# First batch of a decay attention from key-major to query-major tiles, ahead of two feed-forward layers

## The chip, the cores and the metric

The kernel runs on one core of one Trainium2 chip. The metric is device time in microseconds (us), the median of three runs; lower is better. The five instruction queues are PE (TensorE, with its weight loads PEld), DVE (VectorE), ACT (ScalarE), POOL (GpSimd) and SP, which here issues all transfers. Each works through its own list in order.

## What is computed

Four batches of eight heads, 576 tokens, 64 values a head. Attention with a decay and a causal mask is followed by two feed-forward layers on 2304 tokens of 512 values, with 2048 hidden columns each:

```python
scores = scale * np.matmul(q, k.transpose(0, 1, 3, 2))
cum = np.cumsum(np.log(np.clip(f, 0.0001, 1.0)), axis=-1)
decay = cum[:, :, :, None] - cum[:, :, None, :]
scores = np.where(causal, -1000000000.0, scores + decay)
attn = np.exp(scores - np.max(scores, axis=-1, keepdims=True))
attn = attn / (np.sum(attn, axis=-1, keepdims=True) + 1e-09)
x = np.matmul(attn, v)              # then tokens x 512
h = x @ w_in;  g = np.maximum(h, 0.0) + alpha * np.minimum(h, 0.0);  x = g @ w_out
h = x @ w2_in; g = where(h >= 1, h, where(h <= -1, 0, (h + 1) ** 2 / 4)); out = g @ w2_out
```

The inputs q and k are drawn some 29 times larger than a unit scale would ask for, so the scores spread widely, and the row maximum has to be subtracted. The weights come as 64-bit floats.

## The kernel before, in words

**Units.** The attention of a batch is cut into two units: unit 0 holds queries 0 to 255, unit 1 queries 256 to 575 (`QA = 256`). In a unit the eight heads go in four pairs (`pr`). Units 0 and 1, the first batch, are called plain (`plain = u < 2`): their products are fp32 products. The later batches split each operand into a high and a low fp32r part and run each product as two or three fp32r products.

**One head of a plain unit, key-major.** Q and K of the pair are transposed on PE (L573, L538) and copied out by ACT (L582, L546), so that the head's 64 values lie along partitions. L668 multiplies a block of 128 keys with all queries of the unit: a score tile is 128 keys by up to 320 queries. Unit 0 has two such blocks (256 and 128 queries wide, by causality), unit 1 five (320, 320, 320, 192, 64). ACT evacuates each block with the decay of the key as a per-partition bias (L686), POOL masks the diagonal block (L476). The row maximum runs over keys, so along partitions: DVE takes the maximum of the blocks (L707, L725), POOL reduces it over the partitions (L731), DVE subtracts (L747), ACT exponentiates (L752). Keys lie along partitions already, so L787 multiplies V with the probabilities without a transpose. The 64 columns between the two heads of V in `vF` are ones, which gives the sum of each query in a row of the output.

**The normalization.** ACT takes sums and outputs out of PSUM (L829, L830). For each pair SP gathers the sums into 128 partitions (L849), DVE inverts them (L853, L854), SP writes them to DRAM (L857) and reads them back spread over 64 partitions twice (L861), DVE multiplies (L871), and the result is split into its high and low part of x (ACT L881, DVE L884).

**Weights.** `convert` turns each of the 32 pieces of the first layer's 64-bit weights into a high and a low fp32r part: ACT L929, DVE L932, L941, L949, L954, ACT L962, DVE L967, all on 128 x 512. The last two pieces use a buffer of their own (`val1`), one after the other.

**The first layer.** Tokens go in nine chunks of 256, hidden columns in 16 slices. `l1_slice` has twelve products h (L1014), a chain ACT L1024, DVE L1027, ACT L1033, DVE L1036, and twelve products y (L1053) that accumulate over the slices in PSUM; L1068 takes a finished chunk out. Slice s needs the pieces 2s and 2s+1. Chunk 0 needs unit 0 of the first batch, chunk 1 unit 1.

**The order.** Every step is a task with an engine, a cost, a position and its dependencies. `Order.emit` writes the tasks out: at each step it takes the engine that can start first by the planner's own costs, and on it the task with the lowest position (`pos_of` for attention, `l1_pos` for the layer; conversions start 9 positions ahead of their slice). What is written is fixed: on the chip each engine keeps to that order. `phase2` marks the opening of the buffers for the split batches (`open_phase(2)`); it depends on all plain V products and on all 32 conversions:

```python
if u == 2 and pr == 0:
    phase2 = add("X", 0, lambda: open_phase(2), -50, plain_pv + ["convert"])
```

## Time and profile before

| | |
|---|---|
| median of three runs | 1054.39 us |
| lowest and highest | 1053.09 and 1056.34 us |
| profiled execution, first to last instruction | 1054.7 us |
| busy in that span: PE, DVE, ACT, POOL | 1013.4, 752.7, 656.6, 142.0 us |

The profiled execution shows its span, 1054.7 us, as its own time; nothing lies around it that the rows would have to explain. Busy time is the sum of instructions on an engine with overlaps counted once. A span is better read by stage than as a whole, since PE is busy nearly throughout after the first 150 us and is not before.

### The profile page before, as it was taken

What the parts mean: (1) busy time and instruction counts of PE and PEld (TensorE: products, weight loads), DVE (VectorE), ACT (ScalarE), POOL (GpSimd) and SP (SyncE); (2) the same over time, 40 slices, a digit from 0 to 9 for tenths busy, and PEclk for the clock granted to TensorE, in tenths of its full rate; (3) what the DMA queues carried; (4) which work ended last, traced back from release to release, by engine and by line L of the source; (5) the groups of instructions that cost most, each with busy time, mean ns of one, the idle gap of its engine ahead of it and who ended that gap; (6) DMA issues with size and microseconds to landing.
All of it is one profiled execution on the core that took longest, in us unless ns stands there. A gap on an engine that the chain in (4) does not pass through costs nothing.

```text
span 1054.7 us, 18462 instructions
## 1 busy us (share of the span) xinstructions
PE 1013.4 (96%) x6147; PEld 905.4 (86%) x6147; DVE 752.7 (71%) x1899; ACT 656.6 (62%) x1732; POOL 142.0 (13%) x239
## 2 busy tenths in 40 slices
PE   5869979999999999999999999999999999999998
PEld 3548779999999999999999888988888888888886
DVE  7999997888778777787756999974454455444443
ACT  6978867988988788887854655652333343333333
POOL 3422321212331122311200000000000000000000
PEclk9889989999999999999999999999999999999999
DMA  8674422321133111331104454530011001000001
GB/s 229 156 216 113 130 62 55 71 50 49 38 73 72 37 49 38 69 76 37 39 7 129 143 155 148 173 89 32 1 41 40 1 1 40 1 1 31 11 1 40
DMA packets 125071, 72.22 MB, mean 68 GB/s; under 512 B 89360, under 2 KB 118032, under 8 KB 124976
## 3 DMA queue, kind: packets, MB, share of 16 engines
q1 hardware_dynamic: 124976, 71.04, 24.7%
q8 instruction: 49, 0.80, 0.3%
q14 instruction: 46, 0.38, 0.2%
HBM read 61.42 MB, written 9.51 MB: 67 GB/s over the span
## 4 chain that ended last, share of the span: by engine, by line
PE 79%; ACT 7%; DVE 6%; issue 3%; DMA 3%; SPq 1%; POOL 1%; ACTq 0%; POOLq 0%; DVEq 0%
PE ps_h L1287 19%; PE ps_z L1334 19%; PE ps_h L1014 11%; PE ps_y L1053 11%; PE ps_y L1141 4%; PE ps_h L1097 4%; PE ps_s L672 3%; PE ps_o L787 2%; DMA raw<-in_moe_w_in_dram 2%; PE ps_o L793 1%; ACT S L686 1%; ACT S L752 1%; PE ps_o L795 1%; PE ps_o L794 1%; DVE kT L558 1%
## 5 line engine op out<-in xcount | busy, mean ns | idle before, releaser
L1014 PE MATMUL ps_h<-x,w 128*128 128x256 f32 x1344 | 185.3, 288 | 2.4 <-DVE g L1027 2.4
L1053 PE MATMUL ps_y<-gH,w 128*128 128x256 f32 x896 | 184.7, 289 | 0.1
L1287 PE MATMUL ps_h<-xw,w 128*128 128x512 f32 x768 | 184.5, 389 | 0.0
L1334 PE MATMUL ps_z<-w,gH 128*128 128x512 f32 x576 | 177.6, 389 | 0.0
L1014 PEld LDWEIGHTS ps_h<-x,w 128*128 128x128 f32 x1344 | 171.4, 193 | 3.6 <-DVE g L1027 3.5
L1287 PEld LDWEIGHTS ps_h<-xw,w 128*128 128x128 f32 x768 | 144.2, 188 | 29.9
L1312 ACT CAST gH<-g 128x256 fp32r<-128x256 f32 x144 | 58.6, 407 | 166.8 <-PE ps_z L1334 163.3
L1315 DVE TENSOR_TENSOR gL<-g,gH 128x256 fp32r<-128x256 f32 x144 | 61.1, 424 | 128.8 <-ACT gH L1312 128.6
L1053 PEld LDWEIGHTS ps_y<-gH,w 128*128 128x128 f32 x896 | 147.6, 191 | 0.6 <-ACT gH L1033 0.3
L1053 PE MATMUL ps_y<-gL,w 128*128 128x256 f32 x448 | 127.6, 285 | 0.4 <-DVE gL L1036 0.2
L1334 PEld LDWEIGHTS ps_z<-w,gH 128*128 128x128 f32 x576 | 107.2, 188 | 21.5
L1304 ACT ACTIVATE g<-g,half 128x256 f32<-128x256 f32 x144 | 73.2, 509 | 66.4 <-DVE g L1300 66.3
L1334 PE MATMUL ps_z<-w,gL 128*128 128x512 f32 x288 | 112.0, 389 | 0.0
L686 ACT ACTIVATE S<-ps_s,nb 128x320 f32<-128x320 f32 (+3 forms) x224 | 99.6, 449 | 19.3 <-PE ps_s L672 15.6
L476 POOL TENSOR_SCALAR_AFFINE_SELECT S<-S 128x128 f32<-128x128 f32 (+1 forms) x160 | 61.4, 388 | 313.9 <-ACT S L686 262.4
L731 POOL PARTITION_ALL_REDUCE Mb<-Mx x64 | 79.1, 1237 | 77.3 <-ACT Mx L715 43.2
L1307 DVE TENSOR_TENSOR g<-ps_h,g 128x256 f32<-128x256 f32 x144 | 60.9, 424 | 38.8 <-ACT g L1304 38.2
L1053 PEld LDWEIGHTS ps_y<-gL,w 128*128 128x128 f32 x448 | 85.9, 192 | 1.7 <-DVE gL L1036 1.1
L752 ACT ACTIVATE S<-S 128x320 f32<-128x320 f32 (+1 forms) x192 | 79.4, 424 | 12.0 <-DVE S L747 11.2
L747 DVE TENSOR_TENSOR S<-Mb,S 128x320 f32<-128x320 f32 (+3 forms) x224 | 77.5, 397 | 7.0 <-POOL Mb L731 6.0
L787 PE MATMUL ps_o<-S,vF 128*128 128x64 f32 (+4 forms) x256 | 67.4, 357 | 8.8 <-DMA vF<-in_v_dram 4.5
L1027 DVE SCALAR_TENSOR_TENSOR g<-g,calpha,ps_h 128x256 f32<-128x256 f32 x112 | 53.0, 476 | 28.7 <-ACT g L1024 28.2
(112 smaller groups left out, 1799.9 us busy)
## 6 DMA issues: line engine op xcount, KB each, us to landing
raw<-in_moe_w_in_dram SPq DMA_DIRECT2D x32, 512.0 KB
raw<-in_moe_w_out_dram SPq DMA_DIRECT2D x32, 512.0 KB
x<-x SPq DMA_DIRECT2D x9, 512.0 KB
out_dram<-osb SPq DMA_DIRECT2D x18, 256.0 KB
qr<-in_q_dram SPq DMA_DIRECT2D x64, 64.0 KB
raw<-in_k_dram SPq DMA_DIRECT2D x32, 128.0 KB
x<-ysb SPq DMA_DIRECT2D x28, 128.0 KB
raw<-in_v_dram SPq DMA_DIRECT2D x24, 128.0 KB
```

What stands on the lines that cost most here:

```text
L476: nc.gpsimd.affine_select(out=sl, in_=sl, pattern=[[1, sl.shape[1]]], compare_op=ALU.is_ge, fill=NEG, base=base, channel_multiplier=-1)
L686: nc.scalar.activation(out=Sb.t[:, so:so + m], in_=sb.t[:, :m], func=AF.Identity, bias=bias)
L731: nc.gpsimd.partition_all_reduce(Mb.t[:, :n], Mx.t[:, :n], P, ReduceOp.max)
L747: nc.vector.tensor_tensor(out=sl, in0=Mb.t[:, qo:qo + m], in1=sl, op=ALU.subtract)
L752: nc.scalar.activation(out=Sb.t[:, :gn], in_=Sb.t[:, :gn], func=AF.Exp, scale=-SCALE)
L787: nc.tensor.matmul(out=o, lhsT=vf, rhs=Sb.t[:, off - g0:off - g0 + m], start=(kb == 0), stop=last)
L1014: nc.tensor.matmul(out=hb.t, lhsT=a[:, sl], rhs=b, start=(cc == 0 and t == 0), stop=(cc == NCC - 1 and t == 2))
L1053: nc.tensor.matmul(out=Y[c][e // 2][:, e % 2, :], lhsT=a[:, sl], rhs=b, start=(s == 0 and t == 0 and e % 2 == 0), stop=(s == NF - 1 and t ...
L1287: nc.tensor.matmul(out=hb.t, lhsT=a[:, sl], rhs=b, start=(cc == 0 and t == 0), stop=(cc == NCC - 1 and t == 2))
L1304: nc.scalar.activation(out=gb.t, in_=gb.t, func=AF.Square, scale=0.5, bias=half)
L1315: nc.vector.tensor_tensor(out=gg.t[1], in0=gb.t, in1=gg.t[0].bitcast(F32), op=ALU.subtract)
L1334: nc.tensor.matmul(out=zb[tg].t, lhsT=a[:, sl], rhs=b, start=(s == 0 and t == 0), stop=(s == NF - 1 and t == 2))
```

## The change

The first batch gets a function of its own, `plain_pair`, and turns to query-major. A tile is 64 queries of both heads of a pair, 128 rows, by all keys up to the diagonal. Unit 0 has four tiles a pair (64, 128, 192, 256 keys), unit 1 five (320, 384, 448, 512, 576 keys; the last in two parts of 512 and 64). Tiles go in groups of two.

- Q of a tile is laid into a block-diagonal operand of 128 x 128 (L568), scaled by -scale, so one fp32 product (L606) scores both heads. The decay of the keys is added by an fp32r product of a row selector with the high and low parts of the cumulative sums (L608), the triangle by an fp32r product of a matrix holding 2^100 above the diagonal with an identity (L611).
- DVE takes the minimum along the free dimension straight from PSUM (L621). ACT exponentiates from PSUM with the minimum as its bias and adds up each row as it goes (L640). DVE inverts the sums of a group (L663, L664) and scales the probabilities in place (L670). POOL zeroes half a block where a tile ends inside one (L656).
- PE transposes the probabilities block by block (L688), ACT copies four blocks at a time (L693), L701 multiplies V, whose middle columns are zero now, so that both heads accumulate in one output. The result goes straight to its high and low parts (ACT L723, DVE L726).
- Evacuations, masks, partition reductions, subtractions, the two copies of sums and outputs, and the trip of the sums through DRAM go.
- At the start, the cumulative sums are split (ACT L478, DVE L481), and selector, identity and triangle are set up.
- `phase2` waits for the plain products alone, not for the conversions; the last two pieces take their buffers from the ring of K and V (`raw`).

```diff
-        sums=2, rec=2, val1=1, raw2=NRAW, val2=NVAL, x2r=1).items()}
+        sums=2, rec=2, qd0=1, qd1=1, pA=4, pB=3, pt=4, st=3, sw=2, pty=2, raw2=NRAW, val2=NVAL, x2r=1).items()}
...
+    ch = add("ACT", act(S), c_hi, -99, [ft])
+    crow_ready = [ch, add("DVE", dve(S), c_lo, -99, [ch])]
...
+    def plain_pair(u, pr, pos_of, prev_pv):
...
+                nc.scalar.activation(out=qd.t[hr, :nt, hr], in_=pb.t[hr, :n].rearrange("p (t w) -> p t w", w=D),
+                                     func=AF.Copy, scale=-SCALE)
...
+                        nc.tensor.matmul(out=sb.t[:, :w], lhsT=qd.t[:, t, :], rhs=kt.t[:, a0:a1], start=True, stop=False,
+                                         skip_group_check=True)
+                        nc.tensor.matmul(out=sb.t[:, :w], lhsT=sw.t,
+                                         rhs=crow[:, a0:a1], start=False, stop=x < n_ - 1, skip_group_check=True)
+                        if x == n_ - 1:
+                            nc.tensor.matmul(out=sb.t[:, w - D:w], lhsT=identR, rhs=above, start=False, stop=True,
+                                             skip_group_check=True)
...
+                        nc.vector.tensor_reduce(out=stats()[:, 0, 7 - x if x else t:8 - x if x else t + 1], in_=sb.t[:, :w],
+                                                axis=mybir.AxisListType.X, op=ALU.min)
...
+                        nc.scalar.activation(out=pbuf.t[:, a0:a1], in_=sb.t[:, :a1 - a0], func=AF.Exp, scale=-1.0,
+                                             bias=stats()[:, 0, t:t + 1], accum_out=stats()[:, 1, c:c + 1])
...
+                nc.vector.tensor_scalar(out=stats()[:, 2, sl], in0=stats()[:, 1, sl], scalar1=1e-9, scalar2=None, op0=ALU.add)
+                nc.vector.reciprocal(out=stats()[:, 2, sl], in_=stats()[:, 2, sl])
...
+                    nc.vector.tensor_scalar(out=pbuf.t[:, :nkey], in0=pbuf.t[:, :nkey], scalar1=stats()[:, 2, t:t + 1],
+                                            scalar2=None, op0=ALU.mult)
...
+                    for kb_ in kbs:
+                        for pbuf, _, _ in ps:
+                            nc.tensor.transpose(tb.t[:, x:x + P], pbuf.t[:, kb_ * P:(kb_ + 1) * P], ident)
+                            x += P
...
+                    nc.scalar.copy(out=tt.t[:, :w], in_=tb.t[:, :w])
...
+                    for x, kb_ in enumerate(kbs):
+                        for j in range(2):
+                            nc.tensor.matmul(
+                                out=ob.t[:, g * P:g * P + nl * D],
+                                lhsT=V["vF"][:, kb_].rearrange("p a d -> p (a d)")[:, j * D:j * D + P],
+                                rhs=tv[:, x, :, j, :], start=first_ and x == 0 and j == 0,
+                                stop=kb_ == nb_ - 1 and j == 1, skip_group_check=True)
...
+                nc.scalar.copy(out=xt(c)[pr][0][:, x0:x0 + m], in_=ob.t[:, o:o + m])
...
+        if plain:
+            prev_pv = plain_pair(u, pr, pos_of, prev_pv)
+            continue
         if u == 2 and pr == 0:
-            phase2 = add("X", 0, lambda: open_phase(2), -50, plain_pv + ["convert"])
+            phase2 = add("X", 0, lambda: open_phase(2), -50, plain_pv + [a for x in plain_qk for a in x])
...
-        vb = Buf(Ring(1) if there else R["val1" if layer == 1 else "val2"])
+        vb = Buf(Ring(1) if there else R["raw" if layer == 1 else "val2"])
```

**What the order shows on DVE, at the end of unit 0.** Before, the rows around the last x of unit 0, the one that chunk 0 waits for (`raw`, `val` and `w` belong to conversions, `S` and `Mx` to the scores of unit 1):

```order
L747 TENSOR_TENSOR S<-Mb,S 128x64
L941 TENSOR_SCALAR val<-val 128x512
L932 TENSOR_SCALAR val<-val 128x512
L949 SCALAR_TENSOR_TENSOR raw<-raw,val 128x512
L871 TENSOR_TENSOR r<-r,sums 128x256
L725 TENSOR_TENSOR Mx<-S,Mx 128x320
L954 SCALAR_TENSOR_TENSOR raw<-raw 128x512
L884 TENSOR_TENSOR x<-r,x 128x256
```

Now, the same place (`st` holds minima, sums and their inverses, `pp` the probabilities):

```order
L621 TENSOR_REDUCE st<-ps_s 128x1
L1177 SCALAR_TENSOR_TENSOR raw<-raw 128x512
L1164 TENSOR_SCALAR val<-val 128x512
L1172 SCALAR_TENSOR_TENSOR raw<-raw,val 128x512
L663 TENSOR_SCALAR st<-st 128x2
L664 RECIPROCAL st<-st 128x2
L1177 SCALAR_TENSOR_TENSOR raw<-raw 128x512
L670 TENSOR_SCALAR pp<-pp,st 128x320
L726 TENSOR_TENSOR x<-ps_o,x 128x256
```

Before, 13 finished conversions (L967) and the subtractions of two heads of unit 1 stand ahead of that x; now it is 6 finished conversions (L1190) and one scaled tile of unit 1.

**On DVE, at the last conversion.** Before (`val`, the buffer of the last pieces; `g`, `gL` belong to the first layer):

```order
L949 SCALAR_TENSOR_TENSOR val<-raw,val 128x512
L1036 TENSOR_TENSOR gL<-g,gH 128x256
L954 SCALAR_TENSOR_TENSOR val<-raw,val 128x512
L1027 SCALAR_TENSOR_TENSOR g<-g,calpha,ps_h 128x256
L967 TENSOR_TENSOR w<-val,w 128x512
```

Now (`S`, `PL`, `kT`, `q` belong to the second batch):

```order
L1172 SCALAR_TENSOR_TENSOR raw_142<-raw,raw_142 128x512
L979 TENSOR_TENSOR S<-pp,S 128x256
L1177 SCALAR_TENSOR_TENSOR raw_142<-raw,raw_142 128x512
L979 TENSOR_TENSOR S<-pp,S 128x128
L817 TENSOR_TENSOR kT<-pst,kT 64x256
L841 TENSOR_TENSOR q_1711<-pst,q_1711 128x256
L1254 TENSOR_TENSOR gL<-g,gH 128x256
L1190 TENSOR_TENSOR w<-raw_142,w 128x512
```

Work of the second batch, which stood behind the last conversion, stands between its steps now.

**On PE, in unit 0.** The scores, transposes and V products of neighbouring pairs now interleave like this:

```order
L688 MATMUL pst<-ident,pp 128x128 x2
L542 MATMUL pst<-ident,raw_142 128x128 x2
L701 MATMUL ps_o<-S,vF 128x128 x2
L606 MATMUL ps_s<-kT,qd_116 128x64
L608 MATMUL ps_s<-crow,selw 128x64
L611 MATMUL ps_s<-above,identR 128x64
```

Each tile of scores is three products now, and transposes of probabilities (L688) stand ahead of the V products (L701) of the same group. Further down, the first product of chunk 0 (L1014, now L1232) moves from behind the scores of the first two pairs of unit 1 to behind those of its first pair.

## Rows read from the trace of the kernel before

**Rows 1.** Windows of core 0: us, busy per engine (x instructions), PEclk, DMA share, GB/s

```profile
0.00:30.00 30.00, 18.49 (x54) 12.43 (x55) 22.67 (x56) 20.82 (x51) 10.93 (x25) 1.00 0.83 229
30.00:76.00 46.00, 32.04 (x114) 22.68 (x113) 42.99 (x100) 37.10 (x92) 17.32 (x22) 0.78 0.71 189
76.00:140.00 64.00, 59.49 (x376) 50.55 (x374) 62.52 (x155) 53.21 (x133) 18.02 (x25) 0.97 0.37 104
...
300.00:400.00 100.00, 98.78 (x797) 97.54 (x798) 77.24 (x211) 83.54 (x242) 23.05 (x39) 1.00 0.25 56
```

**Rows 2.** Timeline of PE, 22 to 34 us: start, length, instructions [idle before <-releaser]

```profile
22.87 0.63 PE L573 MATMUL pst<-ident,qr 128*128 128x128 f32 x2
23.30 0.63 PE L538 MATMUL pst<-ident,raw 128*128 128x128 f32 x2
...
33.33 0.49 PE L573 MATMUL pst<-ident,qr 128*128 128x128 f32 x3
33.66 0.39 PE L668 MATMUL ps_s<-q,kT 128*128 128x128 f32 x2
```

**Rows 3.** Chain that ended last, 110 to 118 us: start, us, what

```profile
112.90 0.54 PE ps_s L668 x2
...
115.33 1.44 PE ps_y L1053 x12
```

**Rows 4.** Timeline of DVE, 50 to 76 us

```profile
50.33 0.16 DVE L853 TENSOR_SCALAR rec<-rec 128x4 f32<-128x4 f32 x1
50.52 0.18 DVE L854 RECIPROCAL rec<-rec 128x4 f32<-128x4 f32 x1
...
53.29 1.69 DVE L747 TENSOR_TENSOR S<-Mb,S 128x320 f32<-128x320 f32 x5
...
72.25 0.51 DVE L884 TENSOR_TENSOR x<-r,x 128x256 fp32r<-128x256 f32 x1
```

**Rows 5.** Timeline of PE around the end of unit 0 and chunk 0

```profile
50.12 0.63 PE L787 MATMUL ps_o<-S,vF 128*128 128x128 f32 x2
...
75.88 1.32 PE L1014 MATMUL ps_h<-x,w 128*128 128x256 f32 x9
...
166.53 0.28 PE L1053 MATMUL ps_y<-gH,w 128*128 128x256 f32 x1
```

**Rows 6.** Groups of DVE by shape, 0 to 160 us: busy us, mean ns | idle

```profile
L949 DVE SCALAR_TENSOR_TENSOR raw<-raw,val 128x512 int32<-128x512 int32 x30 | 21.9, 731 | 0.2
L967 DVE TENSOR_TENSOR w<-raw,w 128x512 fp32r<-128x512 f32 x30 | 21.6, 721 | 1.4 <-ACT w L962 1.2
...
L941 DVE TENSOR_SCALAR val<-val 128x512 int32<-128x512 int32 x31 | 14.7, 473 | 0.3
L932 DVE TENSOR_SCALAR val<-val 128x512 f32<-128x512 f32 x32 | 14.1, 442 | 3.6 <-ACT val L929 3.5
...
L884 DVE TENSOR_TENSOR x<-r,x 128x256 fp32r<-128x256 f32 x8 | 4.5, 568 | 0.0
```

**Rows 7.** The same groups, 560 to 700 us

```profile
L949 DVE SCALAR_TENSOR_TENSOR val<-raw,val 128x512 int32<-128x512 int32 x32 | 22.0, 686 | 0.2
...
L967 DVE TENSOR_TENSOR w<-val,w 128x512 fp32r<-128x512 f32 x32 | 21.9, 686 | 0.1
...
L932 DVE TENSOR_SCALAR val<-val 128x512 f32<-128x512 f32 x32 | 13.5, 422 | 0.0
L941 DVE TENSOR_SCALAR val<-val 128x512 int32<-128x512 int32 x32 | 13.5, 422 | 0.2
L1125 DVE TENSOR_TENSOR gL<-g,gH 128x256 fp32r<-128x256 f32 x32 | 12.7, 420 | 0.0
```

**Rows 8.** Groups of POOL by shape, 0 to 160 us

```profile
L731 POOL PARTITION_ALL_REDUCE Mb<-Mx x19 | 26.2, 1377 | 29.2 <-ACT Mx L715 17.7 <-DVE Mx L725 8.9 <-DVE raw L954 2.2
L476 POOL TENSOR_SCALAR_AFFINE_SELECT S<-S 128x128 f32<-128x128 f32 x39 | 19.4, 502 | 73.8 <-ACT S L686 67.5 <-PE ps_o L787 6.3
...
L396 POOL MEMSET vF<- 64x64 f32 x2 | 0.4, 298 | 0.1
```

375 lines of the change are left out of this document (265 added, 110 removed).

## The prediction

> **What bounds the kernel now.** I read the busy times by stage first, then the timelines of PE and DVE, then groups of one shape in two stages. The windows [rows 1] show two regimes. From 300 to 400 us PE is busy 98.78 of 100 us: there only PE's work counts. From 76 to 140 us DVE is busy 62.52 of 64 us and PE 59.49. From 30 to 76 us DVE is busy 42.99 of 46 us and PE only 32.04, at a granted clock of 0.78. So the first stage is DVE's: it converts 32 pieces of weights and does its part of attention, PE waits for both. The stage ends where chunk 0 of the first layer ends; its last y products begin at 166.53 [rows 5], and from there PE is nearly saturated. I therefore write the time as (start of the last y of chunk 0) + (work of PE behind it). Before it is 166.5 + 888.2 = 1054.7 us, the profiled execution's own time, 0.3 above the median of the runs, so the sum stands for the median as well.
>
> **Prices.** PE: at the full clock an fp32 product of 320 columns holds PE 0.54 us, twelve fp32r products of 256 columns 1.44 [rows 3]. That is 1.69 ns per fp32 column and 0.12 us per fp32r product of 256 columns. An fp32 transpose holds 0.11 us at 33.33 (three until 33.66), but 0.215 at 22.87 (two until 23.30) [rows 2]: the second is the lower level, 1.2 GHz instead of 2.4, although the window up to 30 us prints a clock of 1.00. DVE: five subtractions with 1216 columns take 1.69 us in a row [rows 4], which fits 0.07 us per instruction, 1.04 ns per column and a tail of 0.08; a scalar operation on 512 columns takes 0.42 against 0.69 for two operands [rows 7], so half the slope.
>
> **PE, added.** 100 transposes at 0.11: 11.0 us. 40 row products of 11,520 columns at 0.12 per 256: 5.4. 36 triangle products of 64 columns: no row shows an fp32r product so narrow; between 0.03 (by columns) and 0.12 (no cheaper than 256 columns) each, 1.1 to 4.3; I take 0.1, 3.6, since the 0.12 row is the only one of that kind. Scores fall from 12,800 fp32 columns to 11,520: -2.2. V products keep 12,800 columns. Sum +17.8 us at full clock, twice that at the low level. In PE's order all of it stands ahead of the last y of chunk 0. There, up to 76 us, PE had 76 - 50.5 = 25.5 us idle [rows 1], and the order lets chunk 0 begin earlier; I cost it at nothing. If that cover is gone, it costs up to 18 us.
>
> **PE, moved.** Since the second batch's buffers no longer wait for the conversions, some of its products come ahead of that last y. Counted in both orders with these prices, 872 us of products stand behind its start before and 868 after: -3.5 us, at the 1.02 us of time per us of priced work (888.2 / 872) that the trace has there.
>
> **DVE, the attention of a pair.** Before, 24 maxima and subtractions of 5248 columns: 7.2 us; two multiplications of 576 columns 0.7; two inversions at 0.34 [rows 4]: 0.7. Sum 8.6. Now ten minima of 2880 columns; no row shows a minimum along a row. By two operands they are 3.7 us, by the scalar slope 2.2, with 0.2 us of extra tail each 5.7; I take 3.7, as a read of one element a cycle is nearest. Nine scalings of 2880 columns at half the slope, with 0.06 for the pointer: 2.7 (4.2 at full slope). Five inversions at 0.34 and two small steps: 1.9. Sum 8.3, so -0.3 a pair, -1.2 us for four. Added at the start: the split of the cumulative sums (0.7) and small copies, +1.2. Ahead of the last conversion stand some 3 us more of the second batch. Net **+3.0 us** of DVE ahead of the last conversion, between -3 and +17 by the bounds.
>
> **POOL, and what it does to DVE.** DVE's conversions are slower in the first 160 us, while POOL works, than between 560 and 700 us, where POOL is idle: 731 against 686 ns, 721 against 686, 473 against 422, 442 against 422 [rows 6, 7]. That is 0.15 us a piece, 4.8 us over 32. The last step into x took 568 ns against 420 for the same shape later [rows 6, 7], 1.2 us over eight; 6.0 in all. Of the time POOL spends in that stage [rows 8], 16 reductions and 32 wide masks are of the first batch, 22.0 + 16.1 us, and eight narrow masks. 20 memsets and 8 selector copies come instead, at the nearest row's 0.3 [rows 8] 8.4 us. So about three quarters of the slowdown goes: **-4.5 us** of DVE (0 to -6.0). The Trainium skill says the same of the cause: GPSIMD Engine Reference, Key points, has POOL share its SBUF interfaces with VectorE and contend with instructions that have two SBUF inputs or run in a 2-port mode. The rows agree for the forms they show.
>
> **ACT, SP, DMA.** ACT loses evacuations and copies, gains PSUM copies of the transposed blocks; it has 37.1 of 46 us busy [rows 1] and ends with less, behind DVE. 32 small transfers go, among them those between the last V product of unit 0 at 50.12 [rows 5] and its last x at 72.25 [rows 4]; no added transfer takes their place. Chunk 0, whose first h begins at 75.88 [rows 5], can start near 55: the order has some 18 us less of DVE work, mostly 7 conversions, ahead of that x. But each slice needs two converted pieces, so this only makes room for PE's extra work and does not by itself move the end of the stage.
>
> **Sum.** The last conversion comes 3.0 - 4.5 = -1.5 us earlier, and with it the last y; -3.5 behind it. 1054.7 - 1.5 - 3.5 = **1049.7 us**. What is late next is PE itself. A measurement of this kernel tells about 0.3% from no change, 3.2 us: faster means below 1051.2, slower above 1057.6.
>
> **Rivals.**
> - *PE pays for its transposes* (no change): PE is 93% busy from 76 to 140 us already [rows 1], and if chunk 0's early start only replaces that work, the 17.8 us eat the 20 gained: 75.9 - 20 + the work from there, 965 us priced against 943, at the 1.037 of today = 1056; with part of the idle time used, 1054. For it: PE's share there. Against it: the 25.5 us idle before.
> - *The stage packs better* (faster still): from 56 us on PE runs at the 1.02 of the later stages: 56 + 965 x 1.02 = 1040. Against it: DVE's conversions, which still need nearly all of its time.
> - *DVE is held at the inversions* (slower): in each of the 20 groups L663 waits until ACT has exponentiated both tiles, and in DVE's own order the next conversions stand behind it; conversions are what the stage waits for. Before, DVE waited little, 3.0 of 46 us and 1.5 of 64 [rows 1]. Each wait adds to the stage whole: 0.25 us in each of 20 takes the 5.0 gained back, 0.8 makes 1049.7 + 16 = 1066.
> - *The clock stays low* (slower): if PE is held at 1.2 GHz up to 76 us, the 17.8 us of new work cost 35.6 and exceed the 25.5 idle by 10: 1049.7 + 10 = 1060. For it: PE runs at the lower level at 23 us between short waits [rows 2]. Against it: at 33.33 transposes run at the full level, and a denser PE waits less. A page speaks for this rival: TensorE: Matmul & The Clock Gate, Part 4: PE-mode transpose, in the Trainium skill says that transposes do not count as busy for the clock as other products do; by it the 100 transposes would not help to raise the clock. The rows here cannot tell, since transposes stand among products.
> - That the change does not do what it says would show as scalings at full slope (+1.5 us a pair, 6 in all); it is in DVE's bounds.
>
> **How the numbers follow.** The forecast has 0.43; its own range, 1045 to 1052, so 0.04 of it counts as no change. Better packing 0.15, PE's payment (no change) 0.19, DVE held 0.15, the low clock 0.08. Faster 0.39 + 0.15 = 0.54, same 0.04 + 0.19 = 0.23, slower 0.23. The range must leave out no more than 0.2: it goes from 1038, under the better packing, to 1063, which takes in the low clock and half of DVE held, whose cost scales with the wait.
>
> **What would show it.** Right: the last conversion some 1.5 us earlier and the last y of chunk 0 near 165; conversion steps on DVE back near 686 and 422 ns; POOL under 20 us before 160; the first h of chunk 0 near 55; PE's busy time in the first 76 us up by 15 us or more; minima of 512 columns near 0.6 us, scalings of 512 near 0.45. Wrong: DVE idle by over 6 us between 30 and 140 us with ACT's exponentials named as releaser (held at the inversions); PE over 95% busy from 60 us on while DVE idles (PE pays); transposes of probabilities at 0.2 us beyond 50 us (the clock); or a gain that sits behind 170 us, which nothing here foresees.

## The result, and the profile after

| | before | after |
|---|---|---|
| median of four runs | 1054.24 us | 1042.41 us |
| lowest and highest | 1053.09, 1056.34 | 1041.90, 1043.20 |
| ratio of the times | | 0.9884, 95% interval 0.9869 to 0.9898 |
| span of the profiled execution | 1054.7 us | 1040.3 us |
| DVE's last conversion (L967, now L1190) starts | 163.3 us | 154.9 us |
| last y of chunk 0 starts (L1053, now L1271) | 168.09 us | 155.04 us |
| span behind that start | 886.6 us | 885.3 us |

The change takes 11.8 us off the medians (12.2 by the ratio); the forecast was 1049.7, inside a range of 1038 to 1063, which is 4.7 below the median of the three runs it knew and 5.0 below the sum it started from. The two spans differ by 14.4. The profiled execution after has a time of 1042.06 for its span of 1040.3, so 1.8 us lie outside the span. The one before is the longest of the four runs, 1056.34 for a span of 1054.7, 2.1 above their median, and the one after is 0.3 below its own: some 2.5 of the 14.4 us are the spread of single executions. So it is not so that nothing lies around the span before, and that the span of 1054.7 comes close to the median of the runs is chance. The sums below go by spans.

The forecast reads the start of the last y of chunk 0 as 166.53 [rows 5]. Each of the 16 slices of a chunk has twelve products y, and 168 = 14 x 12 of them start ahead of 166.53, so the y that begins there is that of the last slice but one. The last one begins 1.6 us later, in the kernel before:

```profile
168.09 0.36 PE L1053 MATMUL ps_y<-gH,w 128*128 128x256 f32 x1
```

The profile after, busy us of each engine, windows as in [rows 1], and one for 140 to 150 us (columns: window and length, then PE, PEld, DVE, ACT, POOL busy with instructions, granted clock, DMA share, GB/s):

```profile
0.00:30.00 30.00, 20.59 (x109) 17.50 (x109) 24.06 (x79) 19.76 (x54) 5.60 (x25) 1.00 0.81 219
30.00:76.00 46.00, 42.84 (x305) 37.21 (x305) 45.21 (x118) 36.31 (x93) 2.25 (x8) 1.00 0.72 196
76.00:140.00 64.00, 62.86 (x481) 57.38 (x480) 62.51 (x156) 45.87 (x119) 6.00 (x19) 1.00 0.35 108
140.00:150.00 10.00, 9.95 (x81) 9.50 (x80) 7.67 (x22) 8.80 (x29) 3.02 (x6) 1.00 0.16 34
300.00:400.00 100.00, 99.63 (x805) 98.98 (x806) 79.62 (x216) 83.24 (x236) 23.06 (x39) 1.00 0.22 51
```

PE gains 10.8 busy us between 30 and 76 us, and the granted clock there is 1.00 instead of 0.78. DVE is as full as before or fuller. ACT has 7.3 us less to do from 76 to 140, and POOL has 8.3 us of work from 30 to 140 instead of 35.3.

DVE's groups by shape up to the end of the last conversion (155.6 us), to be held against [rows 6] and, for the conversion steps without POOL beside them, [rows 7]:

```profile
L1190 DVE TENSOR_TENSOR w<-raw,w 128x512 fp32r<-128x512 f32 x32 | 21.7, 681 | 0.1
L1172 DVE SCALAR_TENSOR_TENSOR raw<-raw,val 128x512 int32<-128x512 int32 x30 | 20.5, 684 | 0.2
L1164 DVE TENSOR_SCALAR val<-val 128x512 int32<-128x512 int32 x30 | 12.5, 419 | 0.2
L1155 DVE TENSOR_SCALAR val<-val 128x512 f32<-128x512 f32 x30 | 12.4, 417 | 0.0
...
L621 DVE TENSOR_REDUCE st<-ps_s 128x1 f32<-128x512 f32 x8 | 5.5, 681 | 0.0
...
L663 DVE TENSOR_SCALAR st<-st 128x2 f32<-128x2 f32 x16 | 2.7, 168 | 0.2 <-ACT pp L640 0.2
...
L670 DVE TENSOR_SCALAR pp<-pp,st 128x512 f32<-128x512 f32 x4 | 1.9, 480 | 0.0
...
L726 DVE TENSOR_TENSOR x<-ps_o,x 128x256 fp32r<-128x256 f32 x8 | 3.3, 414 | 0.0
```

The conversion steps are back at 681 to 684 and 417 to 419 ns. L663 waits 0.2 us in all. POOL's groups up to 160 us, against [rows 8]:

```profile
L963 POOL PARTITION_ALL_REDUCE pp<-pp x5 | 5.8, 1163 | 4.1 <-ACT pp L947 4.1
L505 POOL TENSOR_SCALAR_AFFINE_SELECT S<-S 128x128 f32<-128x128 f32 x12 | 4.3, 364 | 11.1 <-ACT S L918 11.1
L576 POOL CAST selw<-sel 128x128 fp32r<-128x128 f32 x8 | 4.1, 518 | 56.9 <-PE ps_s L611 23.7 <-DVE pp L670 17.0 <-PE ps_s L608 16.2
L656 POOL MEMSET pp<- 128x64 f32 x20 | 3.2, 174 | 42.2 <-PE pst L688 40.5 <-DVE w L1190 1.6
```

PE's timeline in the first batch, and at the end of chunk 0 (start, length, instructions, idle before):

```profile
41.05 0.63 PE L688 MATMUL pst<-ident,pp 128*128 128x128 f32 x4
41.52 0.61 PE L701 MATMUL ps_o<-S,vF 128*128 128x128 f32 x4
...
43.35 1.02 PE L606 MATMUL ps_s<-kT,qd 128*128 128x512 f32 x2
43.81 0.80 PE L608 MATMUL ps_s<-crow,selw 128*128 128x512 f32 x1
44.45 0.19 PE L611 MATMUL ps_s<-above,identR 128*128 128x64 f32 x1
44.48 0.63 PE L542 MATMUL pst<-ident,raw 128*128 128x128 f32 x4
...
46.04 1.61 PE L1232 MATMUL ps_h<-x,w 128*128 128x256 f32 x12
...
155.04 0.28 PE L1271 MATMUL ps_y<-gH,w 128*128 128x256 f32 x1
155.16 0.28 PE L1271 MATMUL ps_y<-gL,w 128*128 128x256 f32 x1
155.63 0.50 PE L1271 MATMUL ps_y<-gH,w 128*128 128x256 f32 x2 [0.19 <-DVE w L1190]
```

Four transposes hold PE 0.47 us (41.05 to 41.52), 0.118 each. The three products of a tile of 512 keys hold it 1.13 us (43.35 to 44.48); the lengths of single records overlap, so the starts count. Chunk 0 begins at 46.0 instead of 75.88 [rows 5], and its last y, begun at 155.04, waits for the last conversion itself (at 155.63).

Up to the end of the last conversion DVE was busy 151.06 of 164.0 us and is now busy 144.86 of 155.6; the last lines of two windows views over just these stretches, before and then after:

```profile
sum 164.00, PE 129.70 PEld 104.94 DVE 151.06 ACT 126.61 POOL 51.10; mean PE 32.42 PEld 26.24 DVE 37.77 ACT 31.65 POOL 12.77
```

```profile
sum 155.60, PE 141.00 PEld 125.72 DVE 144.86 ACT 115.74 POOL 18.64; mean PE 35.25 PEld 31.43 DVE 36.22 ACT 28.94 POOL 4.66
```

So DVE has 6.2 us less work there and 2.2 less idle time, PE does 11.3 us more in 8.4 us less, and ACT has 10.9 us less. DVE's waits for ACT's halves of the conversions in these stretches, two lines before and one after (us in total, times, longest):

```profile
DVE val L932 <- ACT val L929: 3.5, 4, 2.6
DVE w L967 <- ACT w L962: 1.6, 4, 0.8
```

```profile
DVE raw L1155 <- ACT raw L1152: 0.8, 2, 0.5
```

### The profile page after: what moved, and what is told of

Its sections match the earlier page's. It is cut to its first block, busy times and chain, and to the rows that moved or that the text cites. A ratio compares the mean times of both kernels' runs of the same rounds, so it can differ in the third digit from the quotient of the medians.

```text
span 1040.3 us, 18868 instructions
## 1 busy us (share of the span) xinstructions
PE 1017.3 (98%) x6419; PEld 917.7 (88%) x6419; DVE 739.6 (71%) x1910; ACT 639.4 (61%) x1701; POOL 110.0 (11%) x214
## 4 chain that ended last, share of the span: by engine, by line
PE 76%; DVE 13%; ACT 6%; issue 3%; DMA 1%; POOL 1%; SPq 0%; POOLq 0%; ACTq 0%; DVEq 0%
PE ps_h L1505 19%; PE ps_z L1552 19%; PE ps_y L1271 11%; PE ps_h L1232 10%; PE ps_y L1359 4%; PE ps_h L1315 4%; PE ps_s L904 3%; DVE raw L1172 2%; DVE w L1190 1%; DVE raw L1177 1%; PE ps_o L1024 1%; PE ps_o L1018 1%; DVE st L621 1%; PE ps_o L1026 1%; PE ps_o L1025 1%
## 5 line engine op out<-in xcount | busy, mean ns | idle before, releaser
L1271 PE MATMUL ps_y<-gH,w 128*128 128x256 f32 x896 | 183.3, 288 | 0.2 <-DVE w L1190 0.2
L1232 PE MATMUL ps_h<-x,w 128*128 128x256 f32 x1344 | 182.6, 285 | 0.1
L1552 PE MATMUL ps_z<-w,gH 128*128 128x512 f32 x576 | 177.5, 389 | 0.0
L1232 PEld LDWEIGHTS ps_h<-x,w 128*128 128x128 f32 x1344 | 169.0, 190 | 1.4 <-issue 0.9
L1530 ACT CAST gH<-g 128x256 fp32r<-128x256 f32 x144 | 58.6, 407 | 162.9 <-PE ps_z L1552 160.2
L1271 PEld LDWEIGHTS ps_y<-gH,w 128*128 128x128 f32 x896 | 146.6, 190 | 0.7 <-DVE w L1190 0.4
L1271 PE MATMUL ps_y<-gL,w 128*128 128x256 f32 x448 | 126.5, 282 | 0.0
L1271 PEld LDWEIGHTS ps_y<-gL,w 128*128 128x128 f32 x448 | 85.3, 190 | 0.3 <-DVE gL L1254 0.3
L918 ACT ACTIVATE S<-ps_s,nb 128x320 f32<-128x320 f32 (+4 forms) x168 | 75.2, 450 | 9.6 <-PE ps_s L904 8.6
L904 PE MATMUL ps_s<-q,kT 128*128 128x320 f32 (+4 forms) x336 | 72.7, 299 | 3.3 <-DVE kT L817 2.0
L505 POOL TENSOR_SCALAR_AFFINE_SELECT S<-S 128x128 f32<-128x128 f32 (+1 forms) x120 | 42.8, 357 | 237.0 <-ACT S L918 234.4
L1518 DVE TENSOR_SCALAR g<-ps_h 128x256 f32<-128x256 f32 x144 | 60.3, 420 | 7.1 <-PE ps_h L1505 4.9
L984 ACT ACTIVATE S<-S 128x320 f32<-128x320 f32 (+2 forms) x144 | 60.1, 425 | 6.5 <-DVE S L979 5.9
L1552 PEld LDWEIGHTS ps_z<-w,gL 128*128 128x128 f32 x288 | 54.1, 188 | 11.2
```

The costliest lines, as they stand in the source:

```text
L904: nc.tensor.matmul(out=sb.t[:, :m], lhsT=kt.t[:, kb * P:(kb + 1) * P], rhs=qt[t].t[:, qo:qo + m], start=(t == 0), stop=(t == 1))
L918: nc.scalar.activation(out=Sb.t[:, so:so + m], in_=sb.t[:, :m], func=AF.Identity, bias=bias)
L984: nc.scalar.activation(out=Sb.t[:, :gn], in_=Sb.t[:, :gn], func=AF.Exp, scale=-SCALE)
L1232: nc.tensor.matmul(out=hb.t, lhsT=a[:, sl], rhs=b, start=(cc == 0 and t == 0), stop=(cc == NCC - 1 and t == 2))
L1271: nc.tensor.matmul(out=Y[c][e // 2][:, e % 2, :], lhsT=a[:, sl], rhs=b, start=(s == 0 and t == 0 and e % 2 == 0), stop=(s == NF - 1 and t ...
L1518: nc.vector.tensor_scalar(out=gb.t, in0=hb.t[:, hs], scalar1=-1.0, scalar2=1.0, op0=ALU.max, op1=ALU.min)
```

## The experiments

The kernels beginning with `a_` are edits of the changed kernel, those with `b_` of the kernel before. Two marks of each profile, one execution each, tell where the time went: the start of the last conversion on DVE, and the first copy of chunk 0's finished sum out of PSUM (L1068, now L1286), which shows when PE was done with that chunk.

A mark belongs to one execution, which can lie off the median of its kernel: `before` lies 2.1 us above, `b_nopool`, `b_notrip` and `b_act` 1.0 to 1.1 below. Behind the copy of chunk 0 the spans of these four and of `b_dense` agree (885.3 to 886.0 us), so that spread lies ahead of it, where the marks are, and a mark of one of the three is held against one of `before` only to some 3 us. The profiled executions of `after` and the `a_` kernels lie within 0.7 us of their medians, except that of `a_actscale` (1.1 above).

| kernel | median us | ratio to before, 95% | last conversion | chunk 0 out | span |
|---|---|---|---|---|---|
| before | 1054.24 | | 163.3 | 169.1 | 1054.7 |
| after | 1042.41 | 0.9884 (0.9869 to 0.9898) | 154.9 | 157.3 | 1040.3 |
| a_pool | 1049.92 | 0.9947 (0.9935 to 0.9960) | 162.5 | 164.9 | 1048.2 |
| a_tr2 | 1048.88 | 0.9933 (0.9921 to 0.9946) | 161.3 | 163.8 | 1047.1 |
| a_min2 | 1065.91 | 1.0097 (1.0083 to 1.0111) | 178.2 | 180.6 | 1063.4 |
| a_noprod | 1041.42 | 0.9866 (0.9852 to 0.9879) | 153.8 | 156.3 | 1039.6 |
| a_act | 1054.61 | 0.9999 (0.9990 to 1.0007) | 167.6 | 170.0 | 1052.8 |
| a_hop | 1043.67 | 0.9891 (0.9877 to 0.9904) | 155.7 | 158.1 | 1041.8 |
| a_late | 1047.66 | 0.9929 (0.9917 to 0.9941) | 153.8 | 168.9 | 1045.8 |
| a_actscale | 1042.99 | 0.9889 (0.9875 to 0.9902) | 149.2 | 152.3 | 1042.3 |
| a_acthalf | 1046.60 | 0.9925 (0.9912 to 0.9937) | 151.9 | 160.3 | 1044.7 |
| a_scalenoprod | 1042.01 | 0.9876 (0.9856 to 0.9897) | 148.5 | 151.6 | 1039.8 |
| b_nopool | 1052.60 | 0.9973 (0.9958 to 0.9988) | 158.3 | 164.5 | 1049.8 |
| b_open | 1058.16 | 1.0031 (1.0019 to 1.0043) | 167.9 | 177.5 | 1057.1 |
| b_both | 1054.74 | 0.9995 (0.9983 to 1.0007) | 163.1 | 172.7 | 1052.7 |
| b_dense | 1060.91 | 1.0051 (1.0037 to 1.0064) | 167.9 | 173.5 | 1059.5 |
| b_notrip | 1054.19 | 0.9997 (0.9988 to 1.0006) | 160.5 | 165.6 | 1051.4 |
| b_act | 1054.22 | 0.9995 (0.9986 to 1.0004) | 160.2 | 165.7 | 1051.3 |
| b_all | 1052.93 | 0.9982 (0.9972 to 0.9993) | 162.6 | 172.2 | 1051.7 |
| b_four | 1052.00 | 0.9968 (0.9956 to 0.9981) | 155.3 | 166.7 | 1050.3 |

Differences of time below are differences of ratios times 1054.24.

**Load on one engine of the changed kernel.** The theory after the first look: DVE paces the stage, and the time follows the last conversion. POOL work that nobody waits for (`a_pool`), doubled transposes (`a_tr2`), doubled minima (`a_min2`), and PE's products of decay and triangle left out (`a_noprod`):

```diff
+            for x in range(2):
+                add("POOL", 600, lambda: nc.gpsimd.partition_all_reduce(SS[:, 4 * 512:4 * 512 + P], ident, P, ReduceOp.max), pg, sums_)
+            for x in range(2):
+                add("POOL", 350, lambda x=x: causal(SS[:, 4 * 512:4 * 512 + P], 0), pg, sums_)
             def rec(tiles=tiles):
```

> The changed kernel with POOL work put back that nobody waits for: per group of tiles two reductions over partitions and two masks, on a scratch strip, 40 of each, as many masks as the kernel before had; every engine but POOL keeps its order. Theory (DVE paces the first 155 us, and POOL's work slows DVE): the conversion steps go from 681-684 and 417-419 ns back towards 720 and 440-470, some 5 us over 32 pieces and 1 us over the steps into x, the last conversion comes 5 to 7 us later, and the time goes from 1042.4 to 1047-1049. Rival 1 (PE paces, DVE has room): the steps slow down but the time stays within 1 us of 1042.4. Rival 2 (the slow steps before came from something else, such as transfers or ACT): steps stay at 683 and 418 ns, time unchanged.

```diff
+                            for _ in range(2):
                                 nc.tensor.transpose(tb.t[:, x:x + P], pbuf.t[:, kb_ * P:(kb_ + 1) * P], ident)
```

> The changed kernel with each of the 100 transposes of probabilities issued twice into the same place: 11 us more PE work at 0.11 us each, no other engine's list changed. Theory (DVE paces): PE's remaining loss before the last y of chunk 0 takes most of it; 1042.4 becomes 1042 to 1045. Rival (PE paces since the change, 98% busy from 60 us on): the 11 us are paid, 1050 to 1054.

```diff
+                        for _ in range(2):
                             nc.vector.tensor_reduce(out=stats()[:, 0, 7 - x if x else t:8 - x if x else t + 1], in_=sb.t[:, :w],
...
```

> The changed kernel with each of the 40 minima issued twice: 17.9 us more DVE work by the sum of their durations, 10 to 20% of it hidden in overlap, no other engine's list changed. Theory (DVE paces): 1042.4 becomes 1055 to 1060, with the last conversion 13 to 18 us later. Rival (PE paces): DVE's extra work lands in time that PE needs anyway; 1043 to 1048.

```diff
...
-                        nc.tensor.matmul(out=sb.t[:, :w], lhsT=sw.t,
-                                         rhs=crow[:, a0:a1], start=False, stop=x < n_ - 1, skip_group_check=True)
-                        if x == n_ - 1:
-                            nc.tensor.matmul(out=sb.t[:, w - D:w], lhsT=identR, rhs=above, start=False, stop=True,
-                                             skip_group_check=True)
...
```

> The changed kernel without the 40 row products and the 36 triangle products, so decay and causal mask of the first batch are left out: about 9 us less PE work by the forecast's prices, the lists of the other engines unchanged. Theory (DVE paces): 0 to 2 us faster than 1042.4. Rival (PE paces): all of it comes back, 1033 to 1035.

In all four the span moves with the last conversion: +7.6 us there and +7.9 in the span, +6.4 and +6.8, +23.3 and +23.1, -1.1 and -0.7. POOL's work, which nobody waits for, costs 6.6 us; DVE's groups of `a_pool` up to 160 us show how:

```profile
L1196 DVE TENSOR_TENSOR w<-raw,w 128x512 fp32r<-128x512 f32 x31 | 21.5, 696 | 0.1
L1183 DVE SCALAR_TENSOR_TENSOR raw<-raw 128x512 int32<-128x512 int32 x30 | 21.2, 708 | 0.0
L1178 DVE SCALAR_TENSOR_TENSOR raw<-raw,val 128x512 int32<-128x512 int32 x30 | 20.9, 698 | 0.2
L1170 DVE TENSOR_SCALAR val<-val 128x512 int32<-128x512 int32 x30 | 14.2, 476 | 0.2
L1161 DVE TENSOR_SCALAR val<-val 128x512 f32<-128x512 f32 x30 | 14.0, 471 | 0.0
```

Against the changed kernel (681, 683, 684, 419 and 417 ns) that is 15, 25, 14, 57 and 54 ns more a step, some 5 us over 32 pieces: POOL's work slows the steps, as in the kernel before. Neither theory had `a_tr2` right: 11 us of transposes cost 5.2, and they reach DVE: its waits for the scores grow from 1.6 to 5.0 us (waits of DVE up to 155 us, `a_tr2`):

```profile
DVE st L621 <- PE ps_s L611: 5.0, 9, 1.5
```

Taking PE work away (`a_noprod`) shows no difference that the intervals separate. `a_min2` costs more than its work: 17.9 us of minima, 22.5 of time.

**One part of the change in the kernel before.** POOL's work left out (`b_nopool`), the early opening alone (`b_open`), both (`b_both`), and PE kept busy by doubled scores (`b_dense`):

```diff
+                    def mask(Sb=Sb, so=so, w=w, base=base, plain=plain):
-                        causal(Sb.t[:, so:so + w], base)
+                        if not plain:
+                            causal(Sb.t[:, so:so + w], base)
...
+                if plain:
+                    return
                 Mb.t = ap1.tile([P, NMAX], F32, tag=f"M{Mb.slot}", name="Mb")
...
-                        nc.vector.tensor_tensor(out=sl, in0=Mb.t[:, qo:qo + m], in1=sl, op=ALU.subtract)
+                        nc.vector.tensor_tensor(out=sl, in0=sl if plain else Mb.t[:, qo:qo + m], in1=sl, op=ALU.subtract)
```

> The kernel before, with the first batch's reductions over partitions and its masks left out (each subtraction takes the scores from themselves, so the first batch's result means nothing); the lists of the other engines unchanged. Theory (POOL slows DVE, and the time follows the last conversion one to one): conversion steps fall from 731, 721, 471 and 442 ns to near 685, 683, 420 and 418, the last conversion starts 6 to 9 us before 163.3, the time falls by the same, 1054.2 to 1045-1048. Rival (the gain of the change came from elsewhere: PE's fuller clock, the trip through DRAM): steps faster, time within 2 us of 1054.2.

```diff
-            phase2 = add("X", 0, lambda: open_phase(2), -50, plain_pv + ["convert"])
+            phase2 = add("X", 0, lambda: open_phase(2), -50, plain_pv)
...
-        vb = Buf(Ring(1) if there else R["val1" if layer == 1 else "val2"])
+        vb = Buf(Ring(1) if there else R["raw" if layer == 1 else "val2"])
...
```

> The kernel before, with only the opening of the second batch's buffers moved ahead: it no longer waits for the conversions, and the last two pieces take their buffers from the ring of K and V. The PE work behind the last y of chunk 0 falls by 5.5 us by the forecast's prices. Theory: the last conversion starts 2 to 5 us later, as DVE does more of the second batch ahead of it, and 5.6 us go behind it; 1050 to 1054. Rival 1 (it is worth the 3.5 us that the change shows beyond its last conversion, with no price on DVE): 1048 to 1050. Rival 2 (worth nothing): 1054.

`b_both` has both edits above.

> Both edits above together on the kernel before: no reductions and masks in the first batch (its result means nothing), and the early opening. If POOL's quiet and the opening are the whole of the change, this comes to the time of the changed kernel, 1042 to 1046, though it keeps key-major tiles, subtractions and the trip through DRAM. If query-major tiles give something of their own (less DVE work, fewer waits), it stays 3 us or more above 1042.4.

```diff
+                        for _ in range(2):
                             nc.tensor.matmul(out=sb.t[:, :m], lhsT=kt.t[:, kb * P:(kb + 1) * P],
                                              rhs=qt[0].t[:, qo:qo + m], start=True, stop=True)
```

> The kernel before with each score product of the first batch issued twice into the same place: 21.6 us more PE work at 1.69 ns per fp32 column, in the stage where PE idles and its granted clock is 0.78; no other engine's list changed. Rival (the low clock and the idle time themselves cost the 11.8 us): a busier PE keeps its clock and the time falls by 3 us or more. Theory (DVE paces, the clock follows from PE's idling): no gain; between no change and 8 us slower, as DVE waits longer for the scores.

`b_nopool` has the last conversion 5.0 us and the span 4.9 us earlier, with three of its steps at 685 and 686 ns; by the medians the time falls by 2.8, and the rest is the spread of the two executions. `b_open` is slower by 3.3: the last conversion comes 4.6 us later, as DVE splits the second batch ahead of it, and PE's last y 7.5 us behind it instead of 4.8, against 4.9 us less behind that y. Together they are worth 0.5 us, inside the interval. So the two edits on which the forecast's gain stood give key-major tiles next to none of the 12.2 us. `b_dense` has a granted clock of 0.93 between 30 and 76 us and loses 5.4 us: a higher clock that is bought with more work does not pay. No run has the higher clock with the same work, so what the low clock costs is not shown.

**ACT, and the trip through DRAM.** ACT was the next suspect: extra copies on ACT (`a_act`), the trip left out (`b_notrip`), and DVE's scalings moved to ACT, all (`a_actscale`) or 16 of 36 (`a_acthalf`):

```diff
+    nc.gpsimd.memset(SS[:, 2048:2240], 0.0)
...
                         nc.scalar.activation(out=pbuf.t[:, a0:a1], in_=sb.t[:, :a1 - a0], func=AF.Exp, scale=-1.0,
                                              bias=stats()[:, 0, t:t + 1], accum_out=stats()[:, 1, c:c + 1])
+                        for _ in range(2):
+                            nc.scalar.copy(out=SS[:, 2048:2240], in_=SS[:, 2048:2240])
```

> The changed kernel with two copies of 192 columns on a scratch strip behind each of ACT's 40 exponentials, some 20 us of ACT work that nobody waits for; the lists of PE, DVE and SP unchanged. ACT is busy 115.7 us up to the last conversion in the changed kernel, 126.6 in the one before and 133.2 in the one before with POOL quiet and early opening. Theory (ACT's relief is part of the gain: DVE waited for ACT's halves of the conversions): the last conversion comes 4 to 8 us later than 154.9 and DVE's waits on ACT grow from under 3 us to 6 or more; 1046 to 1050. Rival (ACT has room, its load does not matter; the rest of the gain is DVE's own shorter work): 1042 to 1044.

```diff
-        a = add("SP", 620, gather, pn, [a0, a1], new=[db], use=[sb_], move=moved(P, 4 * w))
+        a = a1 if plain else add("SP", 620, gather, pn, [a0, a1], new=[db], use=[sb_], move=moved(P, 4 * w))
+        a = a if plain else add("DVE", 300, invert, pn, [a], use=[db])
...
-        nc.vector.tensor_tensor(out=rb.t[:, :n], in0=rb.t[:, :n], in1=sb_.t[:, :n], op=ALU.mult)
+        nc.vector.tensor_tensor(out=rb.t[:, :n], in0=rb.t[:, :n], in1=(rb if plain else sb_).t[:, :n], op=ALU.mult)
```

> The kernel before without the trip of the first batch's sums through DRAM: no gather, no inversion, no spreading; the multiplication takes the outputs by themselves, so the first batch's result is not normalized. Chunk 0's first h stands some 20 rows earlier in PE's list. DVE loses 3.4 us of inversions. Theory (chunk 0's early start gives PE room but does not move the last conversion): the last conversion 2 to 5 us earlier, the time 1049 to 1053. Rival (chunk 0's start 25 us earlier is the change's gain): 1042 to 1045.

```diff
-                    nc.vector.tensor_scalar(out=pbuf.t[:, :nkey], in0=pbuf.t[:, :nkey], scalar1=stats()[:, 2, t:t + 1],
-                                            scalar2=None, op0=ALU.mult)
+                    nc.scalar.activation(out=pbuf.t[:, :nkey], in_=pbuf.t[:, :nkey], func=AF.Copy,
+                                         scale=stats()[:, 2, t:t + 1])
...
```

> The changed kernel with all 36 scalings on ACT instead of DVE: 14.0 us less DVE work, some 16 us more of ACT's. Theory (DVE paces, and ACT's load counts too): between 8 us faster than 1042.4 and 5 slower, by whether DVE's work or its waits for ACT weigh more. Rival (DVE's work alone counts): 1030 to 1035.

`a_acthalf` has the same edit for the second tile of a group of two.

> The changed kernel with the second scaling of each group of two tiles on ACT: 16 of 36, some 7 us off DVE, some 8 us on ACT. Theory: 1038 to 1043, the better of the two splits if ACT's load counts. Rival (DVE's work alone counts): 1035 to 1037.

Of `a_act`, ACT's group of copies and four of DVE's waits, up to 155 and 165 us. The 80 copies took 349 ns each, 27.9 us instead of the 20 meant, and cost 12.1 us of time:

```profile
L644 ACT COPY S<-S 128x192 f32<-128x192 f32 x80 | 27.9, 349 | 1.3
```

```profile
DVE st L622 <- PE ps_s L612: 3.7, 6, 1.6
DVE x L729 <- ACT x L726: 2.7, 4, 1.1
DVE st L666 <- ACT pp L641: 2.1, 4, 0.8
DVE st L650 <- ACT pp L641: 1.9, 2, 1.0
```

DVE waits for ACT's exponentials and evacuations, and for scores that PE issues late; the last conversion comes 12.7 us later. `b_notrip` starts chunk 0 at 51.8 instead of 75.9 and shows no difference in time (0.3 us). The scalings on ACT bring the last conversion forward (5.7 and 3.0 us), but the span does not follow: no version beats the changed kernel.

**Several parts together in the kernel before.** Exponentials over 64 columns, alone (`b_act`) and on top of `b_both` (`b_all`), and without the trip as well (`b_four`):

```diff
+                    w = D if plain else gn
-                    nc.scalar.activation(out=Sb.t[:, :gn], in_=Sb.t[:, :gn], func=AF.Exp, scale=-SCALE)
+                    nc.scalar.activation(out=Sb.t[:, :w], in_=Sb.t[:, :w], func=AF.Exp, scale=-SCALE)
...
```

> The kernel before with the first batch's exponentials taken over 64 columns of each tile instead of 128 to 320 (the rest is left as it is, so the first batch's result means nothing): some 10.4 us less ACT work, all lists unchanged. Theory (ACT's load delays DVE's conversions, at 0.45 us each as in the changed kernel with added copies): 3 to 5 us faster, 1049.5 to 1051.5. Rival (ACT's load matters only once DVE is faster, or not at all): within 1.5 us of 1054.5.

> The kernel before with no reductions and masks in the first batch, the early opening, and the exponentials over 64 columns (the first batch's result means nothing). Without the last edit it has 1054.7 and its DVE waits 7.1 us for ACT's halves of the conversions. Theory (POOL, ACT and the opening together are the change's gain): 1045 to 1049, the last conversion 6 to 9 us before 163.1. Rival (query-major tiles themselves, with fewer hops and less DVE work, make the gain): 1051 to 1055.

> The kernel before with four edits: no reductions and masks in the first batch, the early opening, exponentials over 64 columns, and no trip of the sums through DRAM (the first batch's result means nothing), so that chunk 0's first h stands 19 rows earlier in PE's list. If the change's gain is these four together: 1043 to 1047. If the tiles themselves matter (score tiles that need one read less on ACT and one hop less, DVE's shorter work): 1049 to 1053.

`b_act` shows no difference in time (0.5 us, inside the interval), so its theory fails; `b_all` gains 1.9 us, which its rival foresaw. `b_notrip` and `b_act` have the last conversion 2.8 and 3.1 us earlier in their profiles, but that is no more than what the executions lie off their medians. In `b_four` the last conversion starts at 155.3, as early as in the changed kernel. But chunk 0 leaves PSUM at 166.7 instead of 157.3, though it begins at 49.8, and the time falls by only 3.4 us. Its windows up to the last conversion:

```profile
0.00:30.00 30.00, 19.48 (x61) 12.95 (x62) 22.97 (x59) 21.73 (x56) 2.00 (x10) 0.89 0.86 237
30.00:76.00 46.00, 38.46 (x217) 29.67 (x217) 43.14 (x108) 40.05 (x112) 0.00 (x0) 1.00 0.68 189
76.00:140.00 64.00, 52.49 (x305) 45.26 (x304) 62.49 (x154) 49.81 (x133) 9.04 (x13) 0.87 0.32 93
140.00:156.00 16.00, 14.14 (x111) 13.04 (x110) 14.99 (x38) 12.82 (x38) 5.65 (x8) 1.00 0.31 82
```

DVE is no longer late; PE is: its last y begins at 164.25, 8.9 us behind the last conversion. It is busy 52.49 of 64 us from 76 to 140, at a clock of 0.87, where the changed kernel has 62.86 at 1.00. The clock is part of this: from 112.2 to 119.0 and from 125.8 to 136.0 it is granted 0.50, the level of 1.2 GHz, and PE is busy 13.4 us there; at the full level that work would take about half, an estimate of 6.7 us less. PE's longest waits, up to 165 us:

```profile
PE ps_y L1060 <- DVE gL L1043: 4.8, 2, 3.8
PE ps_s L668 <- ACT S L686: 3.7, 6, 1.1
PE ps_o L791 <- ACT S L756: 3.6, 2, 3.5
PE ps_s L672 <- DVE qL L602: 3.6, 2, 2.9
```

**What lets PE keep up.** Chunk 0's start held back in the changed kernel (`a_late`), one more handover per tile (`a_hop`), and PE's extra products left out where the scalings are on ACT (`a_scalenoprod`, the edits of `a_actscale` and `a_noprod` together):

```diff
     w_use = {}
+    X_ready[0].append(W_ready[1, 14][1])
```

> The changed kernel with chunk 0's products h held back in the order until the fifteenth piece is converted, near 75 us, where the kernel before begins them; nothing else edited, but the order around them shifts. Forecast's claim (the early start only makes room and does not move the end): within 2 us of 1042.4. Rival (the early start fills PE ahead of a stage in which PE, DVE and ACT are all near full, and is a large part of the gain): 1047 to 1054.

```diff
+                        if x == 0:
+                            nc.gpsimd.tensor_copy(out=stats()[:, 2, t:t + 1], in_=stats()[:, 0, t:t + 1])
                         nc.scalar.activation(out=pbuf.t[:, a0:a1], in_=sb.t[:, :a1 - a0], func=AF.Exp, scale=-1.0,
-                                             bias=stats()[:, 0, t:t + 1], accum_out=stats()[:, 1, c:c + 1])
+                                             bias=stats()[:, 2, t:t + 1], accum_out=stats()[:, 1, c:c + 1])
```

> The changed kernel with each tile's minimum handed on through a copy of one column by POOL ahead of its exponential: 36 tiny POOL copies, some 0.4 to 0.6 us more from minimum to exponential, the lists of PE, DVE, ACT and SP as they are. If the length of the chain of handovers sets the stage: 1046 to 1050, ACT and behind it DVE and PE waiting. If the order has slack for it: 1042 to 1044.

> The changed kernel with the scalings on ACT and without the 40 row and 36 triangle products, so decay and causal mask of the first batch are left out; the lists of all engines but PE as in the kernel with the scalings on ACT (1043.0). Theory (PE's backlog is the limit there): 6 to 9 us off 1043.0, so 1034 to 1037, where the same edit took 1.9 off the changed kernel; the last conversion stays near 149, the rest falls from 893 to 885-887. Rival (something else makes the rest longer): 1040 to 1043.

`a_late`: first the products h of chunk 0 up to 120 us, then the copies of chunk 0's sum (lines of single source lines, with first and last start):

```profile
L1233 PE MATMUL ps_h<-x,w x72: 277/282/367, 72.7 to 114.3; 128*128 128x256 f32 x72
...
L1287 DVE COPY ysb<-ps_y x4: 415/421/426, 168.9 to 238.0; 128x256 f32<-128x256 f32 x4
```

With chunk 0 begun at 72.7 the last conversion comes no later (153.8), yet the last y begins at 166.34, 12.5 us behind it, chunk 0 leaves 11.6 us later, and 4.7 us are lost: the rival's range, at its lower end. The order around the edit shifts too, and 5.8 us of the delay come back behind the last y. `a_hop` shows no difference that the intervals separate: the number of handovers is not what counts, at least where the order was made for one fewer. `a_scalenoprod` refutes its theory: 1.4 us less than `a_actscale`, inside the intervals, so what keeps the versions with scalings on ACT from gaining is not PE's amount of work. Behind the last y their spans are longer, 892.4 (`a_actscale`) and 890.5 us against 885.3; why is open.

## Why the prediction was right and wrong, step by step

**The form of the sum held; its start was read wrongly.** Start of the last y of chunk 0 plus the work behind it: 155.04 + 885.3 after, 168.09 + 886.6 before, where the forecast took the y of the slice ahead of it (166.53). Of the 14.4 us of span, 8.4 lie at the last conversion, where the forecast had 1.5; 4.7 lie between it and the last y, where it had nothing; 1.3 lie behind, where it had 3.5. The 2.5 us by which the two executions lie off their medians are in these numbers, ahead of the last y as far as the runs tell.

**What failed: "ACT, SP, DMA", costed at nothing,** and in it the sentence that chunk 0's early start "only makes room for PE's extra work and does not by itself move the end of the stage". The sum took it over: the last conversion comes earlier, "and with it the last y", as if PE stayed at the same distance. Before, PE's last y begins 4.8 us behind the last conversion; now, with chunk 0 begun at 46.0, it begins 0.1 behind it, and the third of its products waits for it. `a_late` takes the early start away: the last conversion stays, PE falls 12.5 us behind it, and 4.7 us of time go. That both are 4.7 is chance, since `a_late` also moves work from behind that y to ahead of it. So the early start is worth these 4.7 us in the changed kernel. Alone it is not enough: with key-major tiles `b_notrip` begins chunk 0 at 51.8 and `b_four` at 49.8, and their last y still come 3.8 and 8.9 us behind the last conversion.

**The last conversion was mis-sized.** DVE's busy time up to its end falls by 6.2 us, for which the forecast had 1.5, and its idle time by 2.2, for which it had nothing. The terms, each row of DVE counted from its start to the start of the next row or its own end, so that overlaps count once (not listed: the first layer, +0.4, and the set-up, +1.6 where the forecast had +1.2):

- *Attention (-1.2 in four pairs):* 35.8 us before, 31.5 after, so -4.3. A minimum of 512 columns takes 681 ns and a scaling 480, somewhat above the 0.6 and 0.45 foreseen; a scaling of 576 columns takes 513 and one of 64 takes 247, 0.52 ns a column, which refutes the rival that the scalings run at full slope.
- *POOL's contention (-4.5): the right cause, too small.* The conversions hold DVE 88.1 us before and 81.5 after, the steps into x 4.6 and 3.2, 8 us less together; by the plain sum of their lengths the conversions have 98.2 and 92.7, 5.5 less. `a_pool` puts some 5 us of those lengths back and costs 6.6 in all. In the kernel before, the same quiet is worth 2.8 us of time. The Trainium skill's rule cited for it (GPSIMD Engine Reference, Key points) agrees with the runs: the steps with two SBUF inputs lose 2 to 4%, the steps with one input, which run at half the slope, 13 to 14%.
- *The second batch ahead of the last conversion (+3):* 6.0 us before, 10.1 after, so +4.1.
- *ACT "ends with less, behind DVE", at nothing.* In DVE's own list the conversions alternate with steps on ACT. The waits for ACT's halves of the conversions fall from 5.1 to 0.8 us, though other waits take part of it back. In the changed kernel ACT's load is not free: 27.9 us more of it cost 12.1. How much of the 12.2 us its relief gives is not shown: in the kernel before, shorter exponentials (`b_act`) show no difference.

**PE, moved (-3.5): the right way, too large,** with -1.3 behind the last y (-2.6 behind the copy of chunk 0). It is no gain by itself: the same opening in the kernel before has 4.9 us less behind the last y and costs 3.3, through DVE's splits ahead of the conversions and a later PE.

**PE, added (17.8 us, at nothing): right, with little to spare.** The prices hold: 0.118 against 0.11 for a transpose, 1.13 against 0.86 + 0.24 + 0.1 = 1.20 us for a tile of 512 keys. Leaving out products shows no difference, so they are covered; 11 us more cost 5.2, so the cover is used up.

**The rival that came nearest is "the stage packs better", 1040.** What spoke against it, DVE's conversions, was answered by the 8.4 us, and PE, begun on chunk 0 at 46.0, is 98% busy from 76 to 140. Up to the end of the last conversion PE is idle 14.6 us of 155.6 instead of 34.3 of 164.0. That its number is met is in part luck: it starts chunk 0 at 56, and from 46.0 the same sum gives 46 + 965 x 1.02 = 1030.

**The other rivals.** "DVE is held at the inversions" is refuted: 0.2 us. "The clock stays low" is refuted: 1.00 where it was 0.78, with transposes at 0.118 us. The page that spoke for it (the Trainium skill, TensorE: Matmul & The Clock Gate, Part 4: PE-mode transpose) is not decided here: the transposes always have products close by.

**What stays open.** The four parts together give key-major tiles 3.4 of 12.2 us, though the last conversion is as early as with the change. The other 9 are PE's: with key-major tiles it does not have chunk 0 done by then. Whether that comes from the tiles (evacuations that hold score buffers, long V products that wait for one exponential), from the order that was made for them or from the clock was not separated. For the clock speaks that PE worked 28 us at the lower level in the first 155 us before (0.50 granted in seven stretches between 35.5 and 154.9) and 13.4 in `b_four`, and none after, from 20 us on. Against it as the whole: `a_late` has its PE at that level for 3 us only, at 55.6 to 59.0, and its last y comes further behind the last conversion than in any other run.

## What to carry to other kernels

When two engines are both near full in a stage, ask of each change what both do: bringing the last input forward is worth only as much as the other engine has finished by then. An engine that is "behind" the bound in busy time is not free when its steps alternate with the bound's steps in one chain: price its load by adding some and looking. Single parts of such a change, put into the old kernel one by one, need not add up to the change: here one gives 2.8 us, one costs 3.3, two show nothing, and the four together give 3.4 of 12.2. A mark read from one execution is held against another only after both have been held against the medians of their kernels. And which of many equal rows is the last of a chunk is counted, not guessed by its place.

## What was not expected of the hardware

ACT's exponential with a running sum is two instructions: beside each of the 40 exponentials stands a read of the accumulator of 189 to 219 ns, 8 us in all. ACT's copies in place, two behind each other on the same 192 columns, took 349 ns each. POOL's reductions and masks on a strip of their own slowed DVE's steps with one input at half slope by 54 to 57 ns of 418, more than those with two inputs (14 to 25 of 683).
